# The first feed-forward product (f_h) in four groups of 32 array columns

## The chip, the cores and the metric

The kernel runs on one core of one Trainium2 chip. The metric is device time in microseconds (us); times are medians of several runs. The engines are TensorE (PE; its weight loads are shown apart, as PEld), VectorE (DVE), ScalarE (ACT), GpSimd (POOL) and SyncE (SP), which here only issues transfers.

## The reference

Two parts follow each other. A gated linear recurrence over 4 x 8 sequences of 768 steps with 48 features, and a feed-forward block over its 3,072 output rows of 384 features:

```python
for t in range(S):                       # S = 768
    ar, ai = a_re_n[:, :, t, :, None], a_im_n[:, :, t, :, None]
    S_re, S_im = ar * S_re - ai * S_im + kv[t], ar * S_im + ai * S_re     # kv[t] = k_t v_t^T
    y[:, :, t] = einsum('bhd,bhde->bhe', q[:, :, t], S_re)

h = x @ w_in                             # x: y as (3072, 384); w_in: 384 x 1024
e = exp(h - max(h)); sm = e / (sum(e) + 1e-9)
solu = h * sm
ln = (solu - mean) / sqrt(var + 1e-6) * g_ln
out = ln @ w_out                         # 1024 x 384
```

`a_re_n, a_im_n` are the gates with their magnitude held at 0.999. Inputs and output are fp32; the weights come as 8-byte floats and are converted on the chip.

## The kernel before

The 768 steps are cut into 6 chunks of 128, for each of 4 batch entries: 24 chunks, counted with the batch running fastest. Two chunks make a group (`g`), which shares the preparation of the gates. For every chunk n the work is a set of named steps. These put work on TensorE:

- `total` (f_L, L793) and `phase` (f_phase, L847): running sums of the gates' logarithms and angles, 2 products of 128x384 each for a group.
- `score` (f_score, L962): keys by queries, block-triangular, in pieces of 32 keys. `carry` (f_d, L1002): the chunk's contribution to the state. `values` (f_y, L994): the output of the recurrence, by features.
- `up` (f_h, L1034), in two halves: the chunk's 128 tokens by 384 features times `w_in`, 512 of the 1,024 result columns in each half. `xT` (from `turned_x`, L1028, on ScalarE) is the stationary operand, `w_in` streams past it. Three products of 128 features add up in one PSUM bank.
- `down` (f_o, L1110), in two halves of four products: the normalised result times `w_out`.
- `turn_z` (f_zt, L1062): transposes on TensorE for the chunks of `SHORT` (0, 1, 2 and 23). The other chunks are transposed in blocks of 32 by VectorE (`blocks`, f_zb, L1070) and put in place by four transfers (`away`, f_zT, L1075). In the same way `kqb` (f_kb, L915) and `kqt0` (f_kqT, L920) turn keys and queries.

An fp32 product is two pieces in the trace, each with a weight load of its own: a half of `up` shows as 6 pieces, a visit to both halves as 12.

Products use the array in two ways. f_h, f_L, f_phase and f_zt use all 128 columns for one product ("full"). f_score, f_d, f_y and f_o (but for the chunks of `SHORT`) use four groups of 32 columns, each with weights and a range of 32 PSUM partitions of its own ("grouped"); the program issues one product for each group in turn. In f_o:

```python
parts = [(slice(r * 32, r * 32 + 32), st["zT"][:, r, c]) for r in range(4)]
for rows, zT in parts:
    nc.tensor.matmul(out=st["o"][rows], lhsT=zT, rhs=w_out[:, c], start=(c == 0), stop=(c == KF - 1))
```

After `up`, `exp` (ScalarE, L1043) makes z from h; `solu` (VectorE, L1052) multiplies h by z; `centred` and `norm` (GpSimd) and `spread` (ScalarE, L1091) find the mean and the scale; `scale` (ScalarE, L1114) and `store` (SP, L1119) write the output. There is one PSUM buffer for h, of two banks, so the next chunk's `up` waits until `solu` has read h. On VectorE `on` (f_x, L838) joins the angle of the chunk before to this one's and so stands ahead of `phase`; `part` (f_f, L854) follows it; `tot` (L830) reads a small transpose (f_tot, L826); `mask` (f_att, L966) stands ahead of `values`.

The order on every engine is written out by hand: a list of steps for the start, then two lists, `EVEN` and `ODD`, that repeat for n = 2 to 19, and a list for the end. On TensorE one repeat of two chunks is: f_h, f_y, f_o, f_d, f_h, f_score, f_o (half), f_L, f_o (half), f_y, f_score with f_tot, f_phase, f_d.

Of the kernel before, what the change touches and what calls it, by code (L numbers as in the profile page):

```python
# [19 lines left out]
P = 128  # L20
# [549 lines left out]
def whole(ctx, tc, flag, q, k, v, a_re, a_im, moe_w_in, moe_w_out, moe_g_ln, out):  # L570
# [12 lines left out]
    nc = tc.nc  # L583
# [4 lines left out]
    KD = DM // P  # L588
# [23 lines left out]
    w_in = const.tile([P, KD, FF], FP, name="f_w_in")  # L612
# [410 lines left out]
    def ffn_steps(n):  # L1023
        st = {}
# [5 lines left out]
        def up(half):  # L1030
            if half == 0:
                st["h"] = ps_h.tile([P, FF], FP, tag="h", name="f_h")
            for c in range(KD):
                nc.tensor.matmul(out=st["h"][:, half * 512:(half + 1) * 512], lhsT=st["xT"][:, c * P:(c + 1) * P],  # L1034
                                 rhs=w_in[:, c, half * 512:(half + 1) * 512], start=(c == 0), stop=(c == KD - 1))


        def exp():
# [88 lines left out]
        for half in range(2):  # L1127
            own.update({f"up{half}": partial(up, half), f"down{half}": partial(down, half)})
# [127 lines left out]
```

## Time and profile before

| | us |
|---|---|
| median of 3 runs | 443.43 |
| lowest and highest run | 442.80, 444.87 |
| span of the profiled execution | 440.2 |
| PE busy in it | 397.8 |
| DVE busy | 358.8 |
| ACT busy | 286.1 |
| one repeat of two chunks | 31.95 |

The profiled execution's own time is not listed beside its span; the span, from its first to its last instruction, is 3.2 us below the median of the runs. The mean granted TensorE clock is 0.992.

A line of the chain of waits gives start, duration and what ran; there a piece of work is counted from the end of the piece before it. A row of a group of instructions gives line, engine, operation, the tiles written and read, how many, busy time and the mean duration of one. A row of waits gives who waited for whom: total us, times, and the longest.

### The profile page before, as it was taken

The page shows a single profiled execution, that of the slowest core. Times are in us where ns is not written, and L with a number is a line of the kernel's source. Part 1 is how long each engine was busy: PE and PEld are TensorE (multiplying, and loading weights), DVE is VectorE, ACT ScalarE, POOL GpSimd, SP SyncE. Part 2 cuts the span into 40 slices and gives each one's busy share as a digit, 9 for nine tenths or more (in the row PEclk, how much of TensorE's full clock was granted, in tenths as well). Part 3 has the DMA queues.
Part 4 walks back from the last instruction along what each step waited for, and adds up shares of the span by engine and source line. Part 5 has one row for each costly group of instructions (what it writes and reads, how often), then busy time and mean ns, then how long its engine had stood idle before and what let it go on. Part 6 is the DMA issues. An engine that isn't in the chain of part 4 may idle for free.

```text
span 440.2 us, 13458 instructions
## 1 busy us (share of the span) xinstructions
PE 397.8 (90%) x5726; PEld 217.1 (49%) x5726; DVE 358.8 (82%) x540; ACT 286.1 (65%) x453; POOL 52.9 (12%) x149
## 2 busy tenths in 40 slices
PE   0257868999999999999999999999999999999993
PEld 0025424555655645654654654654655646545441
DVE  4798999989799799799799799799898898663220
ACT  4999985986586576666667667657657757703150
POOL 3000020212012011011011011011011011002010
PEclk9999989999999999999999999999999999999998
DMA  8895818588858878888898979789879664474110
GB/s 229 195 268 159 185 25 169 118 185 184 183 115 189 194 166 201 195 195 192 202 205 203 195 174 206 174 189 200 193 173 200 159 156 110 103 175 96 34 58 28
DMA packets 167764, 72.41 MB, mean 164 GB/s; under 512 B 142224, under 2 KB 155536, under 8 KB 167696
## 3 DMA queue, kind: packets, MB, share of 16 engines
q1 hardware_dynamic: 167552, 71.14, 70.4%
q8 instruction: 47, 0.77, 0.7%
q10 hardware_dynamic: 144, 0.33, 0.2%
q14 instruction: 21, 0.17, 0.1%
HBM read 38.87 MB, written 4.72 MB: 99 GB/s over the span
## 4 chain that ended last, share of the span: by engine, by line
PE 83%; ACT 7%; DVE 4%; DMA 2%; SPq 1%; issue 1%; DVEq 0%
PE f_o L1110 29%; PE f_h L1034 27%; PE f_y L994 9%; PE f_score L962 7%; PE f_phase L847 4%; PE f_L L793 3%; PE f_d L1002 3%; DMA f_raw<-in_moe_w_in_dram 1%; ACT f_bits L692 1%; ACT f_bits L694 1%; DMA f_kqT<-f_kb 1%; ACT f_kqT L933 1%; SPq L650 1%; PE f_zt L1062 1%; DVE f_kb L915 1%
## 5 line engine op out<-in xcount | busy, mean ns | idle before, releaser
L1110 PE MATMUL f_o<-f_w_out,f_zT 128*32 128x384 f32 (+1 forms) x1344 | 131.5, 487 | 0.2 <-ACT f_zT L1065 0.2
L1034 PE MATMUL f_h<-f_w_in,f_xT 128*128 128x512 f32 x288 | 130.3, 601 | 0.5 <-ACT f_xT L1028 0.5
L1110 PEld LDWEIGHTS f_o<-f_w_out,f_zT 128*32 128x32 f32 (+1 forms) x1344 | 52.3, 113 | 63.9 <-issue 55.8
L1034 PEld LDWEIGHTS f_h<-f_w_in,f_xT 128*128 128x128 f32 x288 | 52.7, 190 | 60.7 <-issue 57.7
L915 DVE STREAM_TRANSPOSE f_kb<-f_kq 128x1536 f32<-128x1536 f32 x22 | 52.3, 2378 | 2.2 <-DMA f_kqT<-f_kb 1.8
L1052 DVE SCALAR_TENSOR_TENSOR f_z<-f_h,f_z 128x1024 f32<-128x1024 f32 (+1 forms) x36 | 33.6, 966 | 22.0 <-ACT f_z L1043 21.8
L1097 POOL TENSOR_SCALAR f_s<-f_s,f_sum 128x1 f32<-128x1 f32 x24 | 8.1, 338 | 274.2 <-ACT f_z L1091 274.1
L1114 ACT ACTIVATE f_ot<-f_o,f_rs 128x384 f32<-128x384 f32 x24 | 13.9, 581 | 41.1 <-issue 34.9
L962 PEld LDWEIGHTS f_score<-f_kqT 96*32 96x32 f32 x1536 | 31.4, 112 | 14.8 <-issue 8.6
L962 PE MATMUL f_score<-f_kqT 96*32 96x96 f32 (+3 forms) x1536 | 34.9, 239 | 3.3 <-ACT f_kqT L933 1.7
L1043 ACT ACTIVATE f_z<-f_h 128x1024 f32<-128x1024 f32 x24 | 28.5, 1186 | 13.9 <-PE f_h L1034 13.9
L994 PE MATMUL f_y<-f_att,f_v 128*32 128x128 f32 (+1 forms) x384 | 36.4, 274 | 0.5 <-DVE f_state L1014 0.5
L994 PE MATMUL f_y<-f_att,f_vr 128*32 128x128 f32 x384 | 36.2, 274 | 0.0
L793 PE MATMUL f_L<-f_lr,f_mats 128*128 128x384 f32 x48 | 20.0, 541 | 16.7 <-DVE f_lr L788 16.7
L994 PE MATMUL f_y<-f_kqT,f_state 96*32 96x128 f32 (+1 forms) x640 | 32.2, 272 | 0.0
L966 DVE TENSOR_TENSOR f_att<-f_score,f_mats 128x1024 f32<-128x1024 f32 x24 | 29.2, 1215 | 2.9 <-PE f_score L962 2.9
L847 PE MATMUL f_phase<-f_x,f_mats 128*128 128x384 f32 x48 | 21.7, 577 | 6.8 <-ACT f_x L833 6.8
L1091 ACT ACTIVATE f_z<-f_z,f_less 128x1024 f32<-128x1024 f32 x24 | 27.4, 1141 | 0.0
L994 PEld LDWEIGHTS f_y<-f_att,f_v 128*32 128x32 f32 (+1 forms) x384 | 20.8, 102 | 13.4 <-issue 10.3
L850 ACT ACTIVATE f_f<-f_phase,f_bias 128x384 f32<-128x384 f32 x24 | 13.9, 580 | 18.9 <-PE f_phase L847 18.1
L1070 DVE STREAM_TRANSPOSE f_zb<-f_z 128x1024 f32<-128x1024 f32 x20 | 24.7, 1236 | 0.3
L906 DVE TENSOR_TENSOR f_kq<-f_cs,f_k 128x768 f32<-128x768 f32 x24 | 22.9, 953 | 2.1 <-ACT f_cs L864 1.2
(104 smaller groups left out, 611.5 us busy)
## 6 DMA issues: line engine op xcount, KB each, us to landing
f_kqT<-f_kb SPq DMA_DIRECT2D x88, 192.0 KB, 3.3
f_zT<-f_zb SPq DMA_DIRECT2D x80, 128.0 KB, 3.0
f_raw<-in_moe_w_in_dram SPq DMA_DIRECT2D x12, 512.0 KB, 6.1
f_raw<-in_moe_w_out_dram SPq DMA_DIRECT2D x16, 384.0 KB, 5.8
f_ar<-in_a_re_dram SPq DMA_DIRECT2D x12, 384.0 KB, 4.9
f_ai<-in_a_im_dram SPq DMA_DIRECT2D x12, 384.0 KB, 5.4
f_q<-in_q_dram SPq DMA_DIRECT2D x12, 384.0 KB, 4.9
f_k<-in_k_dram SPq DMA_DIRECT2D x12, 384.0 KB, 4.1
```

Source lines behind the costliest of these rows:

```text
L793: nc.tensor.matmul(out=ps, lhsT=tri, rhs=st["lr"][:, i * DM:(i + 1) * DM], start=True, stop=True)
L847: nc.tensor.matmul(out=ps, lhsT=turns, rhs=st["x0"][:, i * DM:(i + 1) * DM], start=True, stop=True)
L915: nc.vector.transpose(out=t, in_=T["kq", c].rearrange("p n h (f j) -> p j (n h) f", j=3))
L962: nc.tensor.matmul(out=scores[r0:r0 + 32, x, r:], lhsT=QK[:, r // 32, x], rhs=QK[:, r // 32:, H + x], start=True, stop=True)
L966: nc.vector.tensor_tensor(out=st["att"].rearrange("p (i u) t -> p i u t", u=2), in0=scores.rearrange("p (i u) t -> p i u t", u=2), in1=mat ...
L994: nc.tensor.matmul(**product)
L1034: nc.tensor.matmul(out=st["h"][:, half * 512:(half + 1) * 512], lhsT=st["xT"][:, c * P:(c + 1) * P], rhs=w_in[:, c, half * 512:(half + 1) ...
L1043: nc.scalar.activation(out=z, in_=h, func=AF.Exp, accum_out=sums[:, n:n + 1])
L1052: nc.vector.scalar_tensor_tensor(out=z, in0=h, scalar=1.0, in1=z, op0=OP.mult, op1=OP.mult, accum_out=st["sum"][:, 2 + i:3 + i])
L1070: nc.vector.transpose(out=st["zb"], in_=st["z"].rearrange("p (c s f) -> p s c f", s=4, f=32))
L1091: nc.scalar.activation(out=st["z"], in_=st["z"], func=AF.Square, bias=st["less"], accum_out=st["sum"][:, 1:2])
L1110: nc.tensor.matmul(out=st["o"][rows], lhsT=zT, rhs=w_out[:, c], start=(c == 0), stop=(c == KF - 1))
```

## The change

`up` makes each product of 128 tokens as four products of 32 tokens: the weight columns `c * P + r` to `c * P + r + 32` of `xT`, into PSUM partitions r to r + 32 of the same two banks. The stream from `w_in` (128 x 512) is the same for all four, so it is issued four times. The order is by feature block c, then by token group r. The flags that start and end the sum over c stay as they are for each group. The order of the steps and all other engines' instructions are unchanged.

```diff
             for c in range(KD):
-                nc.tensor.matmul(out=st["h"][:, half * 512:(half + 1) * 512], lhsT=st["xT"][:, c * P:(c + 1) * P],
-                                 rhs=w_in[:, c, half * 512:(half + 1) * 512], start=(c == 0), stop=(c == KD - 1))
+                for r in range(0, P, 32):
+                    nc.tensor.matmul(out=st["h"][r:r + 32, half * 512:(half + 1) * 512],
+                                     lhsT=st["xT"][:, c * P + r:c * P + r + 32],
+                                     rhs=w_in[:, c, half * 512:(half + 1) * 512], start=(c == 0), stop=(c == KD - 1))
```

## The prediction

> **What bounds the kernel now.** I read the page first, for the busy shares and the chain that ended last.
>
> ```profile
> PE 397.8 (90%) x5726; PEld 217.1 (49%) x5726; DVE 358.8 (82%) x540; ACT 286.1 (65%) x453; POOL 52.9 (12%) x149
> PE f_o L1110 29%; PE f_h L1034 27%; PE f_y L994 9%; PE f_score L962 7%; PE f_phase L847 4%; PE f_L L793 3%; PE f_d L1002 3%; DMA f_raw<-in_moe_w_in_dram 1%; ACT f_bits L692 1%; ACT f_bits L694 1%; DMA f_kqT<-f_kb 1%; ACT f_kqT L933 1%; SPq L650 1%; PE f_zt L1062 1%; DVE f_kb L915 1%
> ```
>
> TensorE carries 83% of the chain, and f_h is 27% of it. A busy share is an average, so next I took one repeat of two chunks, us 217.25 to 249.20, from the table of windows (busy us of PE, weight loads, DVE, ACT, POOL; clock; DMA share; GB/s).
>
> ```profile
> 217.25:249.20 31.95, 31.95 (x520) 17.41 (x514) 29.14 (x40) 21.19 (x33) 3.96 (x11) 1.00 0.89 197
> ```
>
> PE is busy for all of the 31.95 us at full clock, and DVE for 29.14. From 75.2 us to 433.2 us the chain of waits hardly leaves PE. So what a visit to f_h costs on PE is paid in full. The chain, piece by piece (start, us, what), shows what that is; the first seven lines are from inside the steady part and the last five from near its end.
>
> ```profile
> 158.75 1.90 PE f_y L994 x64
> 160.65 5.16 PE f_o L1110 x64
> 165.81 0.68 PE f_d L1002 x48
> 166.49 5.35 PE f_h L1034 x12
> 171.83 1.24 PE f_score L962 x34
> ...
> 179.89 1.76 PE f_y L994 x64
> ...
> 184.54 0.81 PE f_d L1002 x48
> ...
> 373.35 1.10 PE f_score L962 x35
> 374.45 1.51 PE f_phase L847 x4
> 375.96 5.15 PE f_h L1034 x12
> 381.11 1.90 PE f_y L994 x64
> ...
> 392.19 2.93 PE f_o L1110 x31
> ```
>
> f_h, f_phase and f_L use all 128 array columns ("full"); f_y, f_o, f_score and f_d use groups of 32 ("grouped"). Three readings:
>
> - The rate is the same. f_o grouped: 64 pieces in 16 rounds of four take 5.16, 0.3225 us a round for a stream of 384 columns. f_h full: weight loads follow each other every 0.43 us for 512 columns. 0.3225 x 512/384 = 0.430. Twelve of them are 5.15.
> - Entering full from grouped costs 0.20: f_h takes 5.35 after f_d, but 5.15 after f_phase (at 375.96), which is full too.
> - Leaving full costs 0.12 to 0.14, and is booked on the next visit: f_y takes 1.90 after f_h and 1.76 after f_o; f_score 1.24 after f_h and 1.10 after f_y; f_d 0.81 after f_phase and 0.68 after f_o.
>
> So a full visit between grouped ones pays about 0.20 + 0.135 = 0.335 us over its streaming.
>
> **What the Trainium skill says.** "TensorEngine Tiling (Array Packing)", Key Properties: changing the tiling mode, not just the tile, drains TensorE. The trace agrees: in the timeline the loads of f_score begin only 0.94 us after the last load of f_h (inside f_h, 0.43). "TensorE: Matmul & The Clock Gate", Part 3, The mechanism: products on different tiles run at once, with starts about 4 ns apart. In the f_o visit of 224.37 the four of a round start within 21 ns, and a round takes 0.3225 us, the time of one stream. Same page, LDWEIGHTS: time goes by columns, at 1.2 GHz. The rows agree in slope (32 columns 110 ns, 128 columns 190 ns, so 80 ns for 96 columns) but have a fixed part besides.
>
> **The change part by part.**
>
> 1. f_h's products. Per visit, 6 products of 128x512 become 24 of 32x512; each product is two pieces in the trace, so 12 pieces become 48. In four groups they are again 12 rounds of 0.43: 5.15. Nothing gained or lost in the stream. The trace has no 512-column grouped product; the nearest row is f_o's grouped 384-column one. Bounds: +0.02 us a visit if a round costs another 2 ns, and nothing below zero, since 512 columns must be streamed. I take 0.
> 2. Weight loads. 12 of 190 ns become 48 of 110 ns. Cover: the stream of the round before, 430 ns, with four loads abreast; f_o's 64 loads lie under rounds of 322 ns and show no gap on PE. The cover is thin for the first round alone: after f_d the round before lasts only 43 ns, so up to 0.07 us may show. I take 0, and keep 21 x 0.07 = 1.5 for the range.
> 3. Borders removed. Where both neighbours are grouped, 0.335 per visit. Going through the order of visits: chunks 3 to 19, 22 and 23, and three half visits (the second half of chunk 2, both of chunk 21, which stand apart): 22 times.
> 4. A border added. The first half of chunk 2 lies between f_zt and f_phase, both full: +0.335. Chunk 20 follows f_phase and precedes f_y: its one border moves from behind it to ahead of it, 0. Chunks 0 and 1 end in waits of PE for other work (0.9 us and 1.6 us until f_score can start): off the path, 0.
> 5. A wait that grows. The 2.93 at 392.19, for 32 pieces of f_o that take 2.60 elsewhere, holds a wait for the landing of f_zT of chunk 20. Its chain starts at f_phase of 374.45, and between them PE gets 0.335 shorter (the first half of chunk 21). I take that as lost.
> 6. Nothing else moves. The changed program's instruction order has the same instructions with the same waits on DVE, ACT, POOL and SP, and f_h's waits stay on its first products. PE gets 432 more products, 1,728 more records. f_score already starts 128 records in 1.14 us, 9 ns each, and the new f_h visit brings 96 in 5.15: no issue cost.
>
> Sum: (22 - 1 - 1) x 0.335 = 6.7 us. The profiled execution has a span of 440.2; its time with what lies around the span is not given apart. The median of the runs is 443.43, 3.2 more, and I leave that remainder as it is: span 433.5, time **436.7**.
>
> Does the rest keep up? The repeat shrinks by 2 x 0.335 to 31.28. The waits of DVE inside it:
>
> ```profile
> DVE f_tot L830 <- PE f_tot L826: 1.0, 1, 1.0
> DVE f_x L838 <- ACT f_x L833: 0.9, 1, 0.9
> DVE f_f L854 <- ACT f_f L850: 0.7, 2, 0.4
> ```
>
> All three start from PE (f_tot; f_L by way of four exponentials, a table load and the arctangent; f_phase), so they come earlier when PE does. DVE works unbroken from f_tot to the wait for f_x; that wait of 0.92 should shrink by 0.67 to about 0.25. With all three gone DVE could turn in 31.95 - 2.6 = 29.4. Margins of what PE waits for, from the timeline: `on` ends at 245.29 and f_phase starts at 246.89 (1.6, with no f_h between f_L and f_phase to shorten it); attention ready 220.35, f_y at 222.58 (2.2); f_lr ready 237.0, f_L at 239.51 (2.5); f_xT ready 246.09, f_h at 249.19 (3.1). f_zT's last issue of 218.86 lands 2.9 later, and f_o starts at 224.37 (2.6). None loses more than 0.67. SP's queue waits for f_kb 1.5 and for an output tile 1.5 in each repeat, so it has room too. What is late next is `on`.
>
> **The rivals.**
>
> (a) The saving is only part: the first loads after f_d show (-1.5), and the moved edges of transfers and of DVE work cost some hundred ns in several repeats. For: DVE is at 91% of the repeat, DMA at 89%. Against: the margins above. 6.7 less 1.5 to 4: 438 to 441.
>
> (b) No change: DVE becomes the bound and takes it all. It would have to grow from 29.4 to 31.95 of unavoidable time, 9%, and nothing is added to it. Time 443.4.
>
> (c) Slower: the loads of the next round are not hidden. f_h streams 512 columns in four groups at once, a form that the trace lacks. If one load of 110 ns showed in each of 12 rounds, a visit would cost 1.3 - 0.335 more, near 1.0, and 22 of them +21: 465. It decides from 0.335/12 = 28 ns a round on. Against: f_o's weights are 128x32 pieces from SBUF just the same, its stream also comes from a constant weight tile, and its rounds take just what f_h's 430 ns scale to for 384 columns, 322 ns.
>
> (d) The four groups run one after another, or the change is undone on the way to the chip. The first would give 48 x 0.43 = 20.6 us a visit, some 780 in all; f_o's 5.16 for 64 pieces excludes it. The built order shows 24 products of 32x512, which excludes the second.
>
> **How the numbers follow.** A measurement of this kernel tells about 0.5%, 2.2 us, from no change. The forecast, 435.2 to 437.7, has 0.75; (a) 0.14, mostly still faster by over 2.2 us; (b) and other causes of no change 0.05; (c) and other losses 0.06. Faster 0.87, within 0.5% 0.07, slower 0.06. The range must hold 8 in 10: runs of before spread by -0.6 and +1.4 around the median, the first loads may cost 1.5, and part of (a) belongs in it: 435.0 to 440.0.
>
> **What would show it in the profile after.** f_h: 1,152 pieces of 128x32 by 128x512, none as long as 697 ns but behind a full product; a visit of 5.15 in the chain instead of 5.35; f_y after f_h 1.76 and f_score after f_h 1.10; f_d after f_phase still 0.81; the half visit of chunk 2 the one that got slower. The repeat 31.28, PE still busy throughout, DVE's wait for f_x near 0.25. I am wrong if f_h's rounds are over 0.45 us, if PE shows idle time ahead of f_phase, f_y or f_o in every repeat, or if the repeat keeps 31.95.

## The result and the profile after

The changed kernel takes 438.29 us (median of 4 runs, 437.24 to 441.15), the kernel before beside it 443.53 (442.80 to 444.87). The ratio is 0.9894, with a 95% interval of 0.9856 to 0.9932. Run again, unaltered, beside other runs of the kernel before, it took 440.07 (6 runs, 438.02 to 441.86) against 443.97: 0.9899 [0.9862, 0.9937]. The ten runs together have a median of 439.7. The ratios stand as they are on record, with their intervals; they are not the quotients of the medians. So the saving is 4 to 5 us; the forecast said 6.7. The first median and that of the ten runs lie in the forecast's range of 435.0 to 440.0, the second median 0.07 above it.

First the page of the kernel after: the busy line, the queue that brings instructions (transfers, MB, share), and the row of f_h; then the line of that queue in the kernel before.

```profile
PE 392.0 (89%) x6590; PEld 220.2 (50%) x6590; DVE 361.2 (82%) x540; ACT 287.2 (65%) x453; POOL 51.7 (12%) x149
...
q8 instruction: 54, 0.88, 0.9%
...
L1035 PE MATMUL f_h<-f_w_in,f_xT 128*32 128x512 f32 x1152 | 130.4, 593 | 1.1 <-ACT f_xT L1028 1.1
```

```profile
q8 instruction: 47, 0.77, 0.7%
```

f_h has become 1,152 pieces with a mean of 593 ns. TensorE has 6,590 pieces instead of 5,726 and is busy 5.8 us less; DVE's busy time rose by 2.4 us. The instructions come in 54 transfers of 16 KB instead of 47.

One repeat, from the table of windows (PE, weight loads, DVE, ACT, POOL; clock; DMA share; GB/s):

```profile
216.30:247.57 31.27, 31.27 (x591) 17.22 (x586) 29.39 (x41) 21.20 (x33) 3.35 (x11) 1.00 0.88 202
```

31.27 us, where the forecast had 31.28 and the kernel before 31.95. TensorE is still busy throughout. The chain of waits shows the borders. The first two lines are the one place where a border was added; the same place in the kernel before follows in a fence of its own.

```profile
85.99 2.71 PE f_h L1035 x24
88.70 1.49 PE f_phase L847 x4
...
217.85 0.77 PE f_d L1002 x45
218.66 5.15 PE f_h L1035 x47
223.81 1.76 PE f_y L994 x64
...
230.74 0.64 PE f_d L1002 x45
231.42 5.12 PE f_h L1035 x45
236.54 1.14 PE f_score L962 x33
...
240.26 1.49 PE f_L L793 x4
241.75 2.72 PE f_o L1112 x32
...
373.93 5.29 PE f_h L1035 x48
379.22 1.76 PE f_y L994 x64
```

```profile
85.49 2.58 PE f_h L1034 x6
88.07 1.42 PE f_phase L847 x4
```

A visit to f_h after f_d now costs 5.12 to 5.15 (5.35 before). f_y after f_h costs 1.76 (1.90 before), f_score after f_h 1.14 (1.24). The count behind f_h is 45 to 47 and not 48 because its first pieces start among the last ones of f_d, on groups that f_d has finished with (f_h's first starts at 218.42, f_d's last at 218.46): here nothing drains between one step and the next. The half visit of chunk 2 (85.99) rose from 2.58 to 2.71 and f_phase behind it from 1.42 to 1.49, and chunk 20 (373.93), which follows the full f_phase, from 5.15 to 5.29, with f_y behind it down from 1.90 to 1.76.

What did not come out as forecast are a few places where TensorE stands still. They fill most of the next section.

### The profile page after: what moved, and what is told of

Same layout as the page of the kernel before. It is cut to its first block, busy times and chain, and to the rows that moved or that the text cites. A ratio compares the mean times of both kernels' runs of the same rounds, so it can differ in the third digit from the quotient of the medians.

```text
span 438.4 us, 15186 instructions
## 1 busy us (share of the span) xinstructions
PE 392.0 (89%) x6590; PEld 220.2 (50%) x6590; DVE 361.2 (82%) x540; ACT 287.2 (65%) x453; POOL 51.7 (12%) x149
## 4 chain that ended last, share of the span: by engine, by line
PE 73%; DVE 8%; ACT 8%; DMA 5%; issue 3%; SPq 2%; DVEq 0%
PE f_o L1112 26%; PE f_h L1035 22%; PE f_y L994 8%; PE f_score L962 6%; PE f_phase L847 3%; PE f_L L793 3%; PE f_d L1002 3%; DMA f_kqT<-f_kb 3%; DMA f_raw<-in_moe_w_in_dram 2%; SPq L920 1%; ACT f_bits L692 1%; DVE f_kb L915 1%; ACT f_bits L694 1%; DVE f_z L1054 1%; ACT f_kqT L933 1%
## 5 line engine op out<-in xcount | busy, mean ns | idle before, releaser
L1112 PE MATMUL f_o<-f_w_out,f_zT 128*32 128x384 f32 (+1 forms) x1344 | 132.9, 487 | 0.2 <-ACT f_zT L1067 0.2
L1035 PE MATMUL f_h<-f_w_in,f_xT 128*32 128x512 f32 x1152 | 130.4, 593 | 1.1 <-ACT f_xT L1028 1.1
L1112 PEld LDWEIGHTS f_o<-f_w_out,f_zT 128*32 128x32 f32 (+1 forms) x1344 | 60.8, 113 | 56.1 <-issue 46.0
L1035 PEld LDWEIGHTS f_h<-f_w_in,f_xT 128*32 128x32 f32 x1152 | 46.0, 110 | 63.9 <-issue 58.3
L915 DVE STREAM_TRANSPOSE f_kb<-f_kq 128x1536 f32<-128x1536 f32 x22 | 54.3, 2469 | 2.3 <-DMA f_kqT<-f_kb 2.0
L962 PEld LDWEIGHTS f_score<-f_kqT 96*32 96x32 f32 x1536 | 33.0, 112 | 14.5 <-issue 9.9
L962 PE MATMUL f_score<-f_kqT 96*32 96x64 f32 (+3 forms) x1536 | 35.5, 239 | 4.4 <-DMA f_kqT<-f_kb 1.9
L994 PE MATMUL f_y<-f_kqT,f_state 96*32 96x128 f32 (+1 forms) x640 | 34.1, 272 | 0.0
L994 PEld LDWEIGHTS f_y<-f_att,f_v 128*32 128x32 f32 (+1 forms) x384 | 22.6, 103 | 10.4 <-issue 7.7
L847 PE MATMUL f_phase<-f_x,f_mats 128*128 128x384 f32 x48 | 20.5, 549 | 6.8 <-ACT f_x L833 6.8
```

The costliest lines, as they stand in the source:

```text
L847: nc.tensor.matmul(out=ps, lhsT=turns, rhs=st["x0"][:, i * DM:(i + 1) * DM], start=True, stop=True)
L915: nc.vector.transpose(out=t, in_=T["kq", c].rearrange("p n h (f j) -> p j (n h) f", j=3))
L962: nc.tensor.matmul(out=scores[r0:r0 + 32, x, r:], lhsT=QK[:, r // 32, x], rhs=QK[:, r // 32:, H + x], start=True, stop=True)
L994: nc.tensor.matmul(**product)
L1035: nc.tensor.matmul(out=st["h"][r:r + 32, half * 512:(half + 1) * 512], lhsT=st["xT"][:, c * P + r:c * P + r + 32], rhs=w_in[:, c, half * 5 ...
```

## The experiments

All ran beside the kernel before: the first four of the table at its 443.97 us, the next four at 443.93, the last two at 443.70.

| kernel | median us | ratio to before, 95% | undisturbed repeat us |
|---|---|---|---|
| after, again | 440.07 | 0.9899 [0.9862, 0.9937] | 31.27 |
| two groups of 64 columns | 444.04 | 1.0004 [0.9978, 1.0030] | 31.86 |
| records shifted by 128 | 438.74 | 0.9881 [0.9839, 0.9924] | 31.27 |
| f_o's groups reversed | 439.53 | 0.9884 [0.9847, 0.9920] | 31.27 |
| shifted and reversed | 439.82 | 0.9898 [0.9867, 0.9928] | 31.27 |
| f_L and f_phase grouped too | 436.15 | 0.9815 [0.9788, 0.9842] | 30.60 |
| the same, f_o reversed | 436.71 | 0.9838 [0.9798, 0.9878] | 30.60 |
| loops of f_h exchanged | 520.32 (one run) | | 38.33 |
| all grouped, shifted by 64 | 436.55 | 0.9827 [0.9794, 0.9859] | 30.60 |
| all grouped, shifted by 128 | 435.17 | 0.9825 [0.9779, 0.9870] | 30.60 |

The last column is a repeat with no stop or other disturbance in it. Several expected times were missed: three by less than 0.1 us (the second run of the changed kernel, the groups of 64, all grouped and shifted by 64), the others as told below.

### Is it the border, or the smaller pieces?

Two groups of 64 columns are pieces on column groups too, but not the groups that f_d and f_y use.

```diff
-                for r in range(0, P, 32):
-                    nc.tensor.matmul(out=st["h"][r:r + 32, half * 512:(half + 1) * 512],
-                                     lhsT=st["xT"][:, c * P + r:c * P + r + 32],
+                for r in range(0, P, 64):
+                    nc.tensor.matmul(out=st["h"][r:r + 64, half * 512:(half + 1) * 512],
+                                     lhsT=st["xT"][:, c * P + r:c * P + r + 64],
```

> The changed kernel with f_h in two groups of 64 columns instead of four of 32. Borders between column widths as the cause of the gain: f_h still differs from its neighbours of 32 columns, so a visit goes back to about 0.3 us over its stream of 5.15, the repeat of two chunks to 31.8 to 31.95 us, the time to 442.5 to 444. Rival (the gain comes from shorter weight loads or from grouping as such, whatever the width): the repeat stays at 31.3 to 31.5 and the time at 438 to 440.

The chain of this kernel over the same steps, and one repeat:

```profile
218.18 5.30 PE f_h L1035 x24
223.48 1.90 PE f_y L994 x64
...
231.21 5.30 PE f_h L1035 x24
236.51 1.24 PE f_score L962 x34
```

```profile
218.18:250.03 31.85, 31.85 (x539) 16.27 (x541) 29.24 (x40) 21.20 (x33) 4.04 (x11) 1.00 0.86 193
```

f_h takes 5.30 behind f_d, f_y 1.90 and f_score 1.24 behind f_h: the prices of leaving a full product are all back, the one of entering is down by 0.05. The time is that of the kernel before. So what saves is neither small pieces nor column groups as such, but that f_h uses the same 32-column groups as its neighbours. The Trainium skill agrees with this run: "TensorEngine Tiling (Array Packing)" lists 128x64 and 128x32 as configurations of their own (Available Configurations), and changing the mode drains TensorE (Key Properties).

The other way round: if a border costs 0.335, the two steps left with borders, f_L and f_phase, should each give up one.

```diff
-            nc.tensor.matmul(out=ps, lhsT=tri, rhs=st["lr"][:, i * DM:(i + 1) * DM], start=True, stop=True)
+            for r in range(0, P, 32):
+                nc.tensor.matmul(out=ps[r:r + 32], lhsT=tri[:, r:r + 32], rhs=st["lr"][:, i * DM:(i + 1) * DM], start=True, stop=True)
...
-            nc.tensor.matmul(out=ps, lhsT=turns, rhs=st["x0"][:, i * DM:(i + 1) * DM], start=True, stop=True)
+            for r in range(0, P, 32):
+                nc.tensor.matmul(out=ps[r:r + 32], lhsT=turns[:, r:r + 32], rhs=st["x0"][:, i * DM:(i + 1) * DM], start=True, stop=True)
```

> The changed kernel with f_L and f_phase in four groups of 32 columns as well, so that only f_tot (and the ends) still use the full width. Borders as the cause: each of the two visits in a repeat sheds 0.33 us, the repeat falls from 31.27 to 30.6, f_L and f_phase take 1.29 each, and the time falls by 5 to 6 us against the changed kernel, to 432.5 to 435, if VectorE keeps up (its wait ahead of on was 0.34 and goes to about 0). Rival (VectorE or its chain through on becomes the bound): PE shows idle time ahead of f_phase in every repeat and the repeat stays above 30.9, the time at 436 or more.

The chain around f_phase and f_L, one repeat from f_L to f_L, and the waits of DVE in it (who waited for whom: total us, times, longest):

```profile
214.64 1.31 PE f_phase L849 x12
215.95 0.62 PE f_d L1004 x31
...
238.22 1.29 PE f_L L794 x15
239.51 2.58 PE f_o L1114 x31
```

```profile
207.62:238.22 30.60, 30.60 (x614) 16.66 (x609) 29.37 (x39) 20.91 (x34) 3.06 (x11) 1.00 0.89 203
```

```profile
DVE f_tot L831 <- PE f_tot L827: 0.5, 1, 0.5
DVE f_f L856 <- issue: 0.2, 1, 0.2
```

This repeat is 30.60, 0.67 shorter, which is two borders of 0.335. f_L went from 1.49 to 1.29 with 2.58 behind it instead of 2.72; f_phase from 1.51 to 1.31. TensorE is still busy throughout, and DVE, the rival bound, still waits 0.7 in it. The price of a border is thus seen in three steps, undone in one experiment and extended in the other. But not every repeat is like this one. From f_phase to f_phase, between 120 and 339 us, the seven repeats take 30.60 to 32.93, 4.5 us more in all than seven of 30.60. PE's idle time accounts for some 2.8 of that: two stops of the kind shown next (2.4) and a wait for f_kqT (0.5). For the rest the trace shows no wait of PE, and its cause is open. The time, 436.15, missed what was expected for it, 432.5 to 435. This kernel is faster than both; the intervals of its ratio and of that of the changed kernel don't meet.

### Where TensorE stands still without a wait

The timeline of PE in the kernel after, and the pieces of its chain around the second stop ("issue": a wait for nothing that the profile shows):

```profile
118.93 0.77 PE L962 MATMUL f_score<-f_kqT 96*32 96x128 f32 x27
120.42 0.30 PE L962 MATMUL f_score<-f_kqT 96*32 96x96 f32 x5 [0.71 <-issue]
```

```profile
153.47 0.73 PE f_d L1002 x42
154.20 1.23 issue
```

In the middle of a visit PE is idle for 0.71 us in one place and 1.23 in the other, and the trace shows nothing that it waits for. In the second run they are in the same places, with 0.82 and 0.42. Counting PE's records in order of start (a record is one entry of the trace: a product's piece, a weight load or a step of PE's sequencer), the stops lie behind records 2241 and 3521. Both numbers are 193 more than a multiple of 256. An estimate fits this: if a 16 KB transfer of the instruction queue brings 256 records, 1,728 more records need about seven more transfers, as counted. The transfers themselves show the same: the one before each stop ran from 118.12 to 119.00 and from 153.02 to 153.98, and PE went on 1.42 and 1.45 us after it had landed. In the second run these are 1.49 and 1.42. Both had started late: 2.86 and 3.16 us after PE entered the piece of instructions before, where the median of this execution is 0.33. So the fetch came late, and PE ran a piece only some 1.4 us after it had landed.

The same can be read at every boundary between two pieces. With the transfers matched to the boundaries in order, the twelve profiles of this study have 608 of them, and PE passes none sooner than 1.24 us after its transfer has landed. The kernel before comes no nearer than 1.79. Why a transfer starts late is not tested. The steps around the stops (f_score, f_tot, f_phase, f_d) are the densest in records, and at 153.02 two of the four transfers of f_zT were under way.

A theory that can be tried without touching the work: put a few products of no consequence ahead of it, and every boundary falls elsewhere.

```diff
+    extra = ps_t.tile([P, 512], FP, tag="t", name="f_extra")
+    for _ in range(32):
+        nc.tensor.matmul(out=extra[0:1, 0:3], lhsT=ones[:, 0:1], rhs=ones[:, 0:3], start=True, stop=True)
     for s in START.split():
```

> The changed kernel, unaltered, for a second trace and more times. Two theories of the 1.6 us by which it fell short of the forecast. Instruction fetch: PE stops for 0.5 to 1.5 us with no wait shown, at points 256 PE records apart (records of products, weight loads and waits, numbered in order of start: 193 past a multiple of 256, as in the first trace at 2241 and 3521), not in every execution; so this trace has 0 to 3 such stops, each at such a number, and the times spread over 2 to 4 us. Rival: the stops belong to that one execution and to places in the program; then either none here or at other numbers. Skewed groups: from the f_o of chunk 20 on the four groups run out of step until f_zt, the last exponential takes over 2.5 us and f_zt waits 0.5 to 1 us for VectorE, in this trace too; rival: that was chance, and it takes 2.1 us as before. Time 437 to 440.

> The changed kernel with 32 extra products of one column by three (128 PE records) while PE waits at the start; the output does not use them. It moves every later PE instruction by 128 records, half of 256. Instruction fetch: stops without a wait move to numbers 128 on in the program (193 past a multiple of 256 in the numbers of this trace, which count the 128), so not at the second f_score half after 118.9 us nor in f_d at 154 us; most likely about four repeats of two chunks away from there, or none. Time 436.5 to 440. Rival (the stops belong to these places in the program, for example to the transfers issued there): they stay at f_score near 119 and f_d near 154 us.

The waits of PE in the shifted kernel, from 100 us on:

```profile
PE f_o L1112 <- ACT f_zT L1067: 0.2, 1, 0.2
```

Both stops are gone, and no other has come. That alone says little: with f_o reversed (below), where every record keeps its number, the first stop is missing too and the second is 0.14 us, although PE passes these two boundaries 1.48 and 1.46 us after the landing. The profiled execution took 437.77, of which about 1.5 went to a stretch at half the TensorE clock at 75.7 us that the profile of after does not have. But the medians, 438.74 and 440.07, are too close to each other to call on time alone. Nor was it foreseen rightly where another stop would stand: with f_o reversed as well (below) there is one at 186 us, in f_d.

The sharper test is with all steps grouped. There the stops lay behind records 3777 and 8641, with 1.39 and 0.97 us. Shifted by 64 records and by 128:

```diff
+    extra = ps_t.tile([P, 512], FP, tag="t", name="f_extra")
+    for _ in range(16):        # 32 in the second
+        nc.tensor.matmul(out=extra[0:1, 0:3], lhsT=ones[:, 0:1], rhs=ones[:, 0:3], start=True, stop=True)
```

> All 128-column products of a repeat but none of the repeats' order changed: f_h, f_L and f_phase in four groups each, and ahead of the first chunk 16 extra products of 128x1 by 128x3 (64 records of TensorE; their output is used nowhere, nothing else is left out). Theory of the boundaries (TensorE stops with no wait shown where its instruction stream passes from one piece of 256 records to the next while the piece is late): every stop over 0.3 us stands again at a record whose number is 193 more than a multiple of 256, so at places of the program 64 records away from those of the run without the extra products (records 3777 and 8641 there); whether there is a stop at all is a matter of where the boundaries fall in the dense steps. Time 434.0 to 436.5 us, ratio 0.977 to 0.984; the repeat stays at 30.60 us. Rival (the stops belong to places of the program): stops of about 1 us behind the same two products as before, at record numbers 64 higher, 257 less than a full multiple away, time 436.

> As the run with 16 extra products, with 32 of them (128 records of TensorE; their output is used nowhere). Theory of the boundaries: stops over 0.3 us only at records whose number is 193 more than a multiple of 256, so 128 records away in the program from those of the run without extra products; time 434.0 to 436.5 us, ratio 0.977 to 0.984, repeat 30.60 us. Rival (places of the program): the stops behind the same products, at record numbers 128 higher; time 436.

The waits of PE from 75 us on, first shifted by 64, then by 128, and between them the timeline of the longest stop:

```profile
PE f_score L964 <- DMA f_kqT<-f_kb: 4.3, 4, 1.7
PE f_d L1004 <- issue: 3.3, 4, 1.8
PE f_zt L1066 <- DVE f_good L1142: 0.9, 1, 0.9
```

```profile
186.89 0.29 PE L1004 MATMUL f_d<-f_v,f_kq 128*32 128x48 f32 x7 [1.83 <-issue]
```

```profile
PE f_score L964 <- DMA f_kqT<-f_kb: 2.9, 4, 1.6
```

With 64, four stops, behind records 3777, 5057, 9921 and 11201, again all 193 beyond a multiple of 256 and so other products than before; 3.3 us in all. With 128, none over 0.15 us. The profiled executions took 439.84 and 434.45 for the same work; of the 5.4 between them about 3.3 are stops, 1.4 waits for f_kqT and 0.9 the tail (next part). The rival, stops bound to places of the program, is out. Over the twelve profiles there are thirteen such stops, from 0.16 to 1.83 us, every one at 193 beyond a multiple of 256; the kernel before, the one with 64-wide groups and the exchanged loops have none. (Two shorter ones, of 0.13 and 0.14, lie at such numbers as well.) In all thirteen PE goes on 1.24 to 1.54 us after the latest fetch has landed, however long the stop. Whether a boundary stops PE is not settled by its place alone: the changed kernel has some fifty of them and stops at two. Of the medians of the two shifted kernels, 436.55 and 435.17, the first is a hair over the expected 434.0 to 436.5, and their ratios cannot be told apart.

### The tail

At the end, TensorE waits for VectorE in the kernel after; it did not before. The chain of after and of the shifted kernel at that point, and the exponentials in after, in the shifted kernel and in the kernel before (duration ns: lowest, median, highest; the highest is the last one):

```profile
421.52 2.75 DVE f_z L1054 x8
424.44 0.62 PE f_zt L1064 x4
```

```profile
415.94 5.16 PE f_o L1112 x64
421.10 0.60 PE f_zt L1064 x4
```

```profile
L1045 ACT ACTIVATE f_z<-f_h x24: 996/1008/2927, 53.8 to 418.5; 128x1024 f32<-128x1024 f32 x24
```

```profile
L1045 ACT ACTIVATE f_z<-f_h x24: 1001/1008/2085, 52.4 to 416.0; 128x1024 f32<-128x1024 f32 x24
```

```profile
L1043 ACT ACTIVATE f_z<-f_h x24: 1000/1007/2132, 52.3 to 421.3; 128x1024 f32<-128x1024 f32 x24
```

In after the last exponential takes 2,927 ns, 2,132 before; the first two parts of `solu` behind it take 0.88 and 0.87 instead of 0.68 and 0.66, and f_zt starts 0.87 late. From the last f_phase to f_zt it is 52.05 us, no less than the 52.07 before, although the borders between them should give up some 1.0 (four of 0.335, less the one lost to the wait for f_zT); in the shifted kernel it is 50.94. So the tail keeps 1.1 of the saving for itself. One theory: the four groups of columns are out of step when they reach the end. f_o of chunk 20 waits for the landing of one f_zT transfer, and as nothing drains any more, nothing brings the groups together again; the exponential then finds PSUM being written at other moments. Reversing the order of f_o's groups makes the first one wait for the last transfer, and so all.

```diff
-                    parts = [(slice(r * 32, r * 32 + 32), st["zT"][:, r, c]) for r in range(4)]
+                    parts = [(slice(r * 32, r * 32 + 32), st["zT"][:, r, c]) for r in (3, 2, 1, 0)]
```

> The changed kernel with the four groups of f_o issued in the order 3, 2, 1, 0: the group whose transfer lands last waits first, so that all four start together. Skewed groups: the groups stay in step after the f_o of chunk 20, the last exponential takes 2.1 us instead of 2.9, the wait of f_zt for VectorE falls from 0.87 to under 0.3 us, and the time falls by 0.7 to 1.2 us against the changed kernel. Rival (the slow exponential has another cause, such as transfers or VectorE): exponential and wait stay, time the same within 0.3 us.

The last exponential came back to 2,121 ns and the wait for VectorE went away; in its place PE waits 0.49 us for f_zT, in view now. The time, 439.53, is too close to that of the changed kernel to tell. That spoke for the theory. With reversal and shift together:

> Both suspected losses taken away together: the 32 extra products at the start (PE records moved by 128; output unused) and f_o's groups in the order 3, 2, 1, 0. If stops at the ends of instruction pages and the slow last exponential are what the forecast left out, the trace shows neither (no stop without a wait over 0.2 us after 80 us, last exponential 2.1 us, f_zt not waiting), repeats of 31.27 throughout, and the ratio to the kernel before comes to 0.984 to 0.987, the forecast's 0.985. Rival (something else costs the rest): ratio stays near 0.989 although both are gone.

```profile
L1045 ACT ACTIVATE f_z<-f_h x24: 998/1008/3115, 54.8 to 419.2; 128x1024 f32<-128x1024 f32 x24
```

```profile
PE f_zt L1064 <- DVE f_good L1140: 1.1, 1, 1.1
PE f_d L1002 <- issue: 0.8, 1, 0.8
PE f_o L1112 <- DMA f_zT<-f_zb: 0.6, 1, 0.6
```

Here the groups are in step (the last four pieces of f_h start within 0.02 us) and the exponential is the longest of all, 3,115 ns. In the shifted kernel and in the one with all steps grouped they start within 0.18 us, as in the changed kernel, and it takes 2,085 and 2,088. In the shifted and the changed kernel the pieces of f_o that run beside the exponential even start at the same moments of it, to 10 ns. The theory has fallen. The run with both edits also has a stop, behind record 4801, so it says nothing against the boundaries; its ratio, 0.9898, is not the expected 0.984 to 0.987. All grouped, with f_o reversed:

> The same with f_o's groups in the order 3, 2, 1, 0, the candidate for the best version. Borders and skew: repeat 30.6, no skew after late transfers now that hardly any full product brings the groups back in step, last exponential 2.1 us; 0.5 to 1 us below the version without the reversed order, 432 to 434. Rival: the same time as that within 0.3 us.

The exponential took 2,126 ns, PE waited 0.73 us for f_zT, and stops of 0.60 and 1.26 stood behind the same records 3777 and 8641 as without the reversal (which changes no count of records). The time, 436.71, missed the expected 432 to 434. In no pair does the reversal gain anything that the intervals can tell. With all steps grouped and shifted by 64 the exponential takes 2,927 again. It is short or long by some 0.8 us from one kernel to the next; no transfer of data lies in its window and DVE and GpSimd are idle. Its cause stays open.

### Does the order of the groups matter?

f_h with its two inner loops exchanged: all three feature blocks for one group of tokens, then the next group.

```diff
-            for c in range(KD):
-                for r in range(0, P, 32):
+            for r in range(0, P, 32):
+                for c in range(KD):
```

> The changed kernel with the two loops of f_h exchanged: all three feature blocks of one group of 32 tokens, then the next group. If the gain needs four neighbouring products on four different groups, a group's six pieces of a half run one after another and only the first piece of the next group overlaps: 21 rounds of 0.43 instead of 6 for a half, a visit of 18 us instead of 5.15, the time 700 to 730. Rival (PE runs ahead across groups whatever the order): visits of 5.15 and the time as changed.

It took 520.32, far from the expected 700 to 730. One repeat, and PE's timeline at the end of a visit:

```profile
248.15:286.48 38.33, 38.33 (x586) 20.62 (x585) 29.57 (x40) 21.31 (x34) 3.96 (x11) 1.00 0.71 160
```

```profile
255.95 0.30 PE L994 MATMUL f_y<-f_att,f_v 128*32 128x128 f32 x1
...
256.34 0.62 PE L1035 MATMUL f_h<-f_w_in,f_xT 128*32 128x512 f32 x2
...
256.80 0.59 PE L1035 MATMUL f_h<-f_w_in,f_xT 128*32 128x512 f32 x1
...
257.23 0.59 PE L1035 MATMUL f_h<-f_w_in,f_xT 128*32 128x512 f32 x1
```

The repeat is 38.33, 7.06 longer, so 3.5 for each visit: about 8.7 us where one group after another would be 20.6. In the trace each group takes a piece every 0.43 us, but two or three groups run at once, although in the program all six pieces of a group stand ahead of the next group's. And f_y's first piece starts at 255.95, ahead of four pieces of f_h that precede it in the program. The Trainium skill, "TensorE: Matmul & The Clock Gate", Part 3, The mechanism, says that products start and end strictly in the program's order and are never reordered; this trace shows otherwise for the starts of products on different column groups. The look ahead is short, though: the order c, then r, which deals pieces to the four groups in turn, is what makes the change free.

## Why the prediction was right, and where it was off

**What bounds.** Right: PE stayed busy through the repeat, and all that its borders gave up came out of the time.

**Items 1 and 2, stream and weight loads.** Right at 0. Twelve rounds take 5.15 or a little less, and no load shows behind f_d (bound kept for it: 0.07 a visit). The slower rival (c), 28 ns a round, is out. One reading beside it was off without effect: in the f_o visit of 224.37 the four starts of a round lie 5 to 8 ns apart, not about 4.

**Items 3 and 4, borders.** In a repeat right to 0.01 us: 31.27 for 31.28, in the places named (f_y 1.76, f_score 1.14 against 1.10). The added border was put too high: the half visit of chunk 2 and f_phase behind it cost 0.20 more, not 0.335. One detail differs: f_d after f_phase shows 0.77 instead of 0.81, only because f_h's first pieces, which now mix with f_d's last, are booked apart.

**Item 5, a wait that grows.** Near in size, but not where it was put: the f_o visit behind the first half of chunk 21 takes 2.98 instead of 2.93. The loss is spread over the steps behind it. From f_phase of chunk 20 to f_h of chunk 22 the two borders should give up 0.67, and 0.41 came (0.45 in the second execution), so about 0.25 was lost where 0.335 was put.

**Does the rest keep up?** Mostly right. VectorE's wait for f_x, in the steady part from 121 to 377 us, in the kernel before and after:

```profile
DVE f_x L838 <- ACT f_x L833: 9.2, 8, 1.6
```

```profile
DVE f_x L838 <- ACT f_x L833: 3.1, 6, 1.1
```

It fell from 9.2 to 3.1 us over those eight repeats. Where 0.25 was forecast, the last six have 0 to 0.35; in the repeat shown above it is gone. VectorE has a little more to do: its large transposes for f_kb take 2,469 ns in the mean instead of 2,378. But the list of margins left out f_kqT. After the change f_score waits for its landing twice in the first execution, 0.32 us at 108 us and 0.19 at 183, in the second not at all, and in the kernel with all steps grouped and shifted by 64 for 1.28 at 245.

**Item 6 is the step that failed.** "No issue cost" was argued from the rate at which records start inside a visit, 9 ns each. That rate holds. What it left out is that the records have to be brought in: 1,728 more of them are seven more transfers of 16 KB, and at two boundaries the piece came late. Measured: 1.9 us in one execution (0.71 and 1.23) and 1.2 in the other, where the prediction had 0 and no range. That the number of records makes the stops is not shown: the shifted kernel has 128 more and no stop. Shown is that a boundary holds PE up when its piece is late. The second term left out is the tail, 1.1 us: its margins were not looked up. Its cause is open, and the runs show only that it is not there in every kernel of this family.

The sum is taken from the two traces of the changed kernel and the one of the kernel before. For the second execution, from the first f_score of the repeats (75.2 us before, 75.8 after) to the end of the last f_o: 358.00 us before, 354.07 after. That is 3.9 less. Add the two stops with what they held up (1.06 and 0.58 from product to product) and the tail (1.08), and it is 6.65, where the forecast summed 6.7. For the execution of the page: 2.6, and with stops of 0.95 and 1.39, what the waits for f_kqT held up (0.32 and 0.37 from step to step) and a tail of 1.10 it is 6.7. So the mechanism was right, and its size to some tenths. In the shifted kernel, without stops and with the short tail, the same stretch is 5.48 shorter than before, although about 1.5 went to the half clock.

That the time fell into the range is in part luck. The forecast's own 435.2 to 437.7 was missed, and the range reached to 440.0 for first loads that might show; none did, and losses that nobody had listed took their place. The medians, 438.29 and 440.07, lie in the 438 to 441 of rival (a): part of the gain is given back, but not for the reasons named there: no load that shows, but late pieces of the program and a slow tail, and of the edges of transfers only some tenths.

One remainder was misread without effect. The 3.2 us between the span and the median were not all around the span: in the 41 runs of the kernel before that ran beside these experiments, time less span is 1.84 to 2.81. So the profiled execution was a quick one.

What remains between executions of one kernel, about 2 us each way, goes in part with the granted TensorE clock, at half in some stretches of the first 82 us. Of those 41 runs the four with the lowest mean clock, 0.961, took 446.1 to 446.4 us, and those with 0.992 or more 441.8 to 444.0. In the ten runs of the changed kernel no such order shows: the quickest, 437.24, had 0.972.

## What to carry to other kernels

When a step's neighbours run on groups of 32 columns, a full-width product between them pays for two switches, here 0.335 us together. Splitting it into four products of the same stream, dealt to the groups in turn, cost nothing here, where the stream of a round takes 430 ns and a load 110 ns, and a 64-wide split beside groups of 32 saved nothing. Instructions have to be brought in, too: count the records, look for idle time of the engine with no releaser in the middle of a visit, and see whether its record numbers share a remainder. Before a sum is made, list the margin of every buffer that the bounding engine reads, the tail's too.

## What the runs showed of the hardware that was not expected

- Thirteen stops of TensorE, 0.16 to 1.83 us, all at records 193 beyond a multiple of 256, each ending 1.24 to 1.54 us after the landing of a 16 KB piece of instructions, whose transfer took 0.88 to 0.96 us. None of 608 such boundaries was passed sooner after the landing.
- Products on different column groups overtake each other in start, over step borders too; f_h with exchanged loops ran up to three groups at once.
- The same exponential of 128x1024 from PSUM took 2,085 to 3,115 ns in the tail from kernel to kernel, with nothing in the trace to tell the long from the short.
- VectorE's transposes of 128x1536 took 2,378 ns in the mean in the kernel before, 2,469 with f_h grouped, 2,585 with all steps grouped, but 2,385 with the loops of f_h exchanged. So grouping alone does not lengthen them; the cause is open.
